# Sparse attention and a fast-multiplied MLP on one core: all steps behind batch 0 dealt in a new order

## The chip, the cores and the metric

The kernel runs on one core of one Trainium2 chip. A core has engines that run their own instruction rows side by side: TensorE (PE, with its weight loads as PEld), VectorE (DVE), ScalarE (ACT), GpSimd (POOL) and SyncE (SP). They wait for each other through semaphores, and 16 DMA engines move data for all of them. The metric is the device time of one execution in microseconds; lower is better.

## The reference

Attention with fixed sparse masks over 8 batches and 8 heads (576 tokens, 64 per head), then an MLP over all 4608 tokens. Heads 0 to 3 see the last 32 positions ("local"), heads 4 to 7 every 32nd position back from their own ("strided").

```python
B, H, S, D = 8, 8, 576, 64
scores = q @ k.T / sqrt(D)
local   = (rel >= 0) & (rel < 32)              # heads 0..3
strided = (rel >= 0) & (pos_k % 32 == pos_q % 32)  # heads 4..7
attn = softmax(where(mask, scores, -1e9))
x = (attn @ v).transpose(0, 2, 1, 3).reshape(4608, 512)
h = x @ w_in                                   # 512 -> 2048
g = h * tanh(softplus(h))                      # Mish
out = g @ w_out                                # 2048 -> 512, float32
```

## The kernel before

The tokens are cut into 9 tiles of 512 for the MLP, while attention goes by batches of 576. Stage t (there are 10) does three things at once: the first matrix product of tile t, the second product of tile t - 1, and the attention of batch t + 1. Tile 0 multiplies plainly in part; all else uses a scheme with seven products of half-size blocks instead of eight, for which DVE makes sums of blocks: `wis` and `wos` of the weights (once), `xs` of the tokens, `gs` of the activated values.

Nothing decides the order while the program runs or is built: ten strings of words (`PLANS`, from line 735) are gone through one after the other, and `do` (line 624) turns each word into instructions. An engine's row is the order in which its words stand in the strings. The order between words of different engines has no effect of its own; it decides only which instruction must wait for which. A last letter A or D names the engine, ACT or DVE; `@b` names a batch; `^` and `_` take the tile after or before the stage's own.

The words that matter here:

- `ld:..` loads k, q and v (`ks`, `kl`, `qs`, `ql`, `vs`, `vl`: s for strided, l for local heads) by DMA from POOL, `wo` and `wi` parts of the weights.
- `T:..` and `t:..`: batches 0 to 2 have q and k transposed on TensorE (T), and a copy (t) to `kTs`, `qTs`, `kTl`, `qTl`. From batch 3 on `D:..` does it by DMA transpose from SP.
- `q`, `e`, `k`, `v`, `r`: scores, exponential (ACT), mask (DVE), PV product, norm (DVE, lines 314 and 319). `sp` spreads V of the strided heads (`vs`), `sh` copies 32 rows of V of the local heads to the neighbour block (`vl`, line 182).
- `X`, `Y`, `xc`, `yc`, or by DMA transpose `y` and `V` with a copy `vc`: the attention's result transposed into `xT`.
- `x:0..3` the sums xs; `1:g` to `7:g` the seven products of column group g; `1c`, `5c` copies, `6c`, `7c` sums between them (`ee`, `hh`); `E`, `H`, `Z` the activations (lines 449, 451, 453).
- `m1` to `m7` the seven products of the second matrix, in halves; `n` and `g:1..3` the sums gs; `st` the stores from SP; `p1`, `pm`, `p2`, `oc` the plain form of tile 0.
- `hold`: a tiny copy on POOL that waits for a DMA transpose, so that the loads behind it in POOL's row don't start before.

The two lines through which every order of this change goes:

```python
        for t, plan in enumerate(PLANS):
            go(plan, t)
```

Of the kernel before, what the change touches and what calls it, by code (L numbers as in the profile page):

```python
# [45 lines left out]
def kernel(ctx, tc, q, k, v, moe_w_in, moe_w_out, out):  # L46
    nc = tc.nc
    B, H, S, D = q.shape
# [24 lines left out]
    hold = sb([1, 2], "hold")  # L73
# [9 lines left out]
    vs = sb([128, 4, CS, VD], "vs")  # L83
# [488 lines left out]
    with tc.manual_schedule():  # L572
# [158 lines left out]
        def go(plan, t=0):  # L731
            for w in plan.split():
# [26 lines left out]
            ),  # L759
            (  # L760
# [7 lines left out]
            ),  # L768
            (
# [9 lines left out]
            ),  # L779
            (  # L780
# [8 lines left out]
            ),  # L789
            (  # L790
# [8 lines left out]
            ),  # L799
            (  # L800
# [7 lines left out]
            ),  # L808
            (
# [7 lines left out]
            ),  # L817
            (
# [51 lines left out]
```

## Time and profile before

| | us |
|---|---|
| median of 3 runs | 284.81 |
| the three runs | 289.52, 284.75, 284.81 |
| the profiled execution | 284.39 |
| its span, first to last instruction | 282.6 |
| DMA queue q0 (loads from POOL) | 57808 packets, 18.30 MB |
| DMA queue q1 (transposes and stores from SP) | 40112 packets, 18.32 MB |

The profile is of one execution. "Busy" counts the time in which an engine worked on an instruction; "idle before" an instruction is the time its engine stood still ahead of it, with what ended it. Matmuls are pipelined: one that is listed with 0.27 us can follow the one ahead after 0.11. The rows themselves stand in the prediction, each where it is used.

### The profile page before, as it was taken

The numbers are of one execution on the slowest core, as the hardware profiler recorded it, in microseconds if no ns is written. First come the engines' busy times: TensorE is split into PE (matmuls) and PEld (weight loads), VectorE is DVE, ScalarE is ACT, GpSimd is POOL, SyncE is SP. The second block draws the span as 40 slices with busy tenths as digits, with TensorE's granted clock in tenths as the row PEclk, the third lists the DMA queues.
The fourth block names the chain that finished last, engine by engine and source line by source line (L and its number), as shares of the span: only waits on it lengthen the run. The fifth ranks groups of instructions, "written<-read, shape, count | busy, mean of one in ns | idle before, by whom it ended". The sixth has DMA issues, their size and how long they took to land.

```text
span 282.6 us, 7628 instructions
## 1 busy us (share of the span) xinstructions
PE 273.8 (97%) x3241; PEld 227.0 (80%) x3241; DVE 223.6 (79%) x381; ACT 189.4 (67%) x286; POOL 57.5 (20%) x78
## 2 busy tenths in 40 slices
PE   8999999999999999999999999999899999999994
PEld 3657745668989898998898889888789888888883
DVE  3679868999979886989699888886988766758761
ACT  2576884699968778788956876788376528613711
POOL 8533440250009005400720072002000000000000
PEclk9999999999999999999999999999999999999999
DMA  7999999999838978999899989999353003002104
GB/s 148 189 206 201 205 186 197 98 223 123 149 73 103 141 143 122 240 132 163 164 195 123 151 212 162 107 166 209 56 169 57 15 2 148 2 1 106 45 2 148
DMA packets 98242, 37.35 MB, mean 132 GB/s; under 512 B 79800, under 2 KB 93688, under 8 KB 98208
## 3 DMA queue, kind: packets, MB, share of 16 engines
q0 software_dynamic: 57808, 18.30, 63.9%
q1 hardware_dynamic: 40112, 18.32, 28.8%
q8 instruction: 25, 0.41, 0.6%
q10 hardware_dynamic: 288, 0.25, 0.3%
q14 instruction: 9, 0.07, 0.1%
HBM read 37.05 MB, written 9.44 MB: 164 GB/s over the span
## 4 chain that ended last, share of the span: by engine, by line
PE 84%; DVE 6%; DMA 5%; POOL 2%; issue 1%; ACT 1%; DVEq 0%; ACTq 0%; POOLq 0%
PE set L121 51%; PE ee L121 20%; PE at L121 7%; DMA w_in<-in_moe_w_in_dram 5%; PE at L302 4%; DVE xs L115 1%; DVE wis L115 1%; PE at L349 1%; DVE wos L115 1%; POOL w_in L173 0%; PE ee L349 0%; DVE qTl L112 0%; DVE ee L115 0%; DVE osb L112 0%; POOL vl L160 0%
## 5 line engine op out<-in xcount | busy, mean ns | idle before, releaser
L121 PEld LDWEIGHTS <-wis 128*128 128x128 bf16 x577 | 55.6, 98 | 10.9 <-issue 2.8
L121 PEld LDWEIGHTS <-gs 128*128 128x128 bf16 x512 | 49.2, 98 | 6.2
L121 PEld LDWEIGHTS <-gT 128*128 128x128 bf16 x448 | 42.3, 98 | 9.7 <-issue 0.3
L121 PEld LDWEIGHTS <-w_in 128*128 128x128 bf16 x436 | 41.2, 97 | 7.9 <-issue 1.0
L121 PE MATMUL set<-w_out,gT 128*128 128x256 bf16 (+1 forms) x304 | 46.3, 295 | 0.3 <-ACT gT L453 0.3
L121 PE MATMUL set<-xT,w_in 128*128 128x256 bf16 (+1 forms) x264 | 39.9, 275 | 0.6 <-DMA w_in<-in_moe_w_in_dram 0.2
L453 ACT ACTIVATE gT<-set 128x1024 bf16<-128x1024 f32 x32 | 32.8, 1024 | 11.1 <-PE set L121 10.5
L121 PE MATMUL set<-xs,wis 128*128 128x256 bf16 x256 | 37.9, 272 | 0.3 <-DVE ee L115 0.2
L449 ACT ACTIVATE gT<-ee 128x512 bf16<-128x512 f32 x35 | 20.4, 596 | 11.9 <-PE ee L121 11.1
L121 PE MATMUL set<-wos,gs 128*128 128x256 bf16 x224 | 27.6, 273 | 0.0
L115 DVE TENSOR_TENSOR ee<-set,hh 128x512 f32<-128x512 f32 x32 | 22.3, 696 | 5.8 <-PE set L121 3.4
L115 DVE TENSOR_TENSOR hh<-set,hh 128x512 f32<-128x512 f32 x32 | 21.9, 685 | 4.1 <-PE set L121 4.0
L110 ACT COPY set<-set 128x512 f32<-128x512 f32 x31 | 17.9, 579 | 9.0 <-PE set L121 8.1
L451 ACT ACTIVATE gT<-hh 128x512 bf16<-128x512 f32 x35 | 21.7, 629 | 3.2 <-DVE hh L115 3.2
L115 DVE TENSOR_TENSOR gs<-gT,gs 128x2048 bf16<-128x2048 bf16 x16 | 19.5, 1220 | 3.7 <-issue 1.7
L121 PE MATMUL ee<-xs,wis 128*128 128x256 bf16 x140 | 21.0, 272 | 0.0
L121 PE MATMUL ee<-xT,wis 128*128 128x256 bf16 x140 | 20.8, 273 | 0.0
L115 DVE TENSOR_TENSOR gs<-gT 128x2048 bf16<-128x2048 bf16 x16 | 19.4, 1214 | 1.1 <-ACT gT L451 1.1
L121 PE MATMUL set<-xs,w_in 128*128 128x256 bf16 x128 | 19.2, 272 | 0.3 <-DVE hh L115 0.3
L319 DVE TENSOR_TENSOR x_s<-at,rden 72x768 bf16<-72x768 f32 (+1 forms) x22 | 18.8, 857 | 0.8
L110 ACT COPY osb<-set 128x1024 f32<-128x1024 f32 (+1 forms) x8 | 7.7, 960 | 15.8 <-PE set L121 15.8
L110 ACT COPY hh<-ee 128x512 f32<-128x512 f32 x24 | 14.1, 588 | 5.9 <-PE ee L121 5.9
(144 smaller groups left out, 461.8 us busy)
## 6 DMA issues: line engine op xcount, KB each, us to landing
out_dram<-osb SPq DMA_DIRECT2D x17, 512.0 KB, 3.4
vl<-in_v_dram POOLq DMA_DIRECT2D x8, 288.0 KB, 12.8
w_out<-in_moe_w_out_dram POOLq DMA_DIRECT2D x4, 512.0 KB, 14.6
ks<-in_k_dram POOLq DMA_DIRECT2D x7, 288.0 KB, 12.1
qs<-in_q_dram POOLq DMA_DIRECT2D x7, 288.0 KB, 10.6
vraw<-in_v_dram POOLq DMA_DIRECT2D x7, 288.0 KB, 6.7
w_in<-in_moe_w_in_dram POOLq DMA_DIRECT2D x3, 512.0 KB, 15.4
kl<-in_k_dram POOLq DMA_DIRECT2D x10, 144.0 KB, 10.4
```

What stands on the lines that cost most here:

```text
L110: Sc.copy(out_, in_)
L115: eng.tensor_tensor(out=out_, in0=a, in1=b, op=op)
L121: PE.matmul(o, lhsT=lhsT, rhs=rhs, start=start, stop=stop, skip_group_check=True)
L302: PE.matmul(po[:, e, i, :] if kind == "l" and self.apart else po[:, (n - n0) // per, (n - n0) % per, :], lhsT=pt[0:r, c0:c0 + 128], rhs=rh ...
L319: Dv.tensor_tensor(out=xo, in0=po[0:m, :, :, 0:D], in1=rd.unsqueeze(3).to_broadcast([m, nb, per, D]), op=ALU.mult,)
L349: PE.transpose(tr[:, n * j:n * j + n], x[0:n, u:u + 2, :].rearrange("p u d -> p (u d)"), ident[0:n, 0:n],)
L449: Sc.activation(o[:, 0:2, 256:512], two(E), AF.Mish)
L451: Sc.activation(o[:, 2:4, 256:512], two(h[:, 1, :]), AF.Mish)
L453: Sc.activation(o[:, :, 0:256].rearrange("p (b u) n -> p b u n", b=2), pair[:, 0:2, :].rearrange("p b (u n) -> p b u n", u=2), AF.Mish,)
```

## The change

Strings 0 (from its middle, behind batch 0) to 9 are replaced. The same words stand in both, each as often; their order differs, and some copies and sums carry another engine letter. Counted over the program, DVE has three copies fewer and ACT three more. The rows of TensorE hold the same 3241 matmuls in another order. POOL's and SP's rows read the same before and after, word for word. In the code nothing else differs. Of the strings, a line or two is enough; this is the start of stage 6:

```diff
-                "m1:1 m1c:D m5:0 _H:3 g:1 _Z:3 ae vc:1:D@6 q:l1:F e:l1:F q:l0:A e:l0:A m5:1 m5c:A m6:0 m6:1 m6c:A g:2 "
-                "k:l0:D vc:0:D@6 x:0 q:s2:F _y:1 _y:0 _hold x:1 k:l1:D q:l2:A q:s0:A e:s0:A m3:0 e:l2:A m2:1 g:3 "
-                "e:s2:F 1:0 1c:0:A q:s1:A m7:1 x:3 m7:0 sh:D _st:1 m7c 5:0 e:s1:A v:l0:A r:l0:A am 6:0 m4:0 m4:1 "
...
+                "m5:0 m5:1 _E:3 m2:0 m2:1 _H:3 q:l1:F q:l0:A g:1 m6:0 g:2 sh:D ae e:l1:F m6:1 k:l1:D _V m5c:A m3:0 "
+                "e:l0:A q:l2:A q:s0:A q:s2:F m6c:A e:s0:A g:3 k:l0:D m7:1 e:l2:A e:s2:F q:s1:A vc:1:D@6 1:0 m7:0 "
+                "e:s1:A _y:1 _y:0 vc:0:D@6 x:0 5:0 k:l2:D 1c:0:A v:l0:A x:1 6:0 m7c m4:0 _hold m4:1 k:s0:D x:2 m3:1 "
```

DVE's row at that place, before. The two copies `xT<-ks` are vc:1 and vc:0, `gs` are the sums g, `Pl` masks, `xs` the sums x, and `vl` is sh, the copy of V rows:

```order
L115 TENSOR_TENSOR gs<-gT,gs 128x2048
L112 COPY xT<-ks 128x576
L115 TENSOR_TENSOR gs<-gT 128x2048
L280 TENSOR_TENSOR Pl_88<-Pl_88,consts_sb 128x2x480
L112 COPY xT<-ks 128x576
L115 TENSOR_TENSOR xs<-xT 128x512
L115 TENSOR_TENSOR xs<-xT,xs 128x512
L280 TENSOR_TENSOR Pl_89<-Pl_89,consts_sb 128x2x480
L115 TENSOR_TENSOR gs<-gT,gs 128x2048
L115 TENSOR_TENSOR xs<-xT,xs 128x512
L112 COPY vl_80<-vl_80 32x4x5x64
```

And now:

```order
L115 TENSOR_TENSOR gs<-gT,gs 128x2048
L115 TENSOR_TENSOR gs<-gT 128x2048
L112 COPY vl_80<-vl_80 32x4x5x64
L280 TENSOR_TENSOR Pl_89<-Pl_89,consts_sb 128x2x480
L115 TENSOR_TENSOR gs<-gT,gs 128x2048
L280 TENSOR_TENSOR Pl_88<-Pl_88,consts_sb 128x2x480
L112 COPY xT<-ks 128x576 x2
L115 TENSOR_TENSOR xs<-xT 128x512
L280 TENSOR_TENSOR Pl_90<-Pl_90,consts_sb 128x2x192
L115 TENSOR_TENSOR xs<-xT,xs 128x512
```

The copy of V rows has moved from behind both xT copies to well ahead of them, and both xT copies behind all gs sums and two masks.

ACT's row at the end of tile 0, before (`gT` rows are activations, of which the last `gT<-set_102` is Z of group 3; `set_102` is a copy 1c, `kTs` a copy t of batch 1, `Ps` an exponential):

```order
L110 COPY set_102<-set_102 128x512
L110 COPY kTs<-at 128x8x72
L451 ACTIVATE gT<-hh_68 128x2x256
L453 ACTIVATE gT<-set_103 128x4x256
L451 ACTIVATE gT<-hh_69 128x2x256
L449 ACTIVATE gT<-ee_105 128x2x256
L449 ACTIVATE gT<-ee_104 128x2x256
L451 ACTIVATE gT<-hh_68 128x2x256
L453 ACTIVATE gT<-set_102 128x4x256
L691 ACT_TABLE_LOAD
L274 ACTIVATE Ps_85<-at 72x2x144
```

And now:

```order
L110 COPY kTs<-at 128x8x72
L110 COPY set_102<-set_102 128x512
L110 COPY kTs<-at 128x8x72
L453 ACTIVATE gT<-set_103 128x4x256
L110 COPY qTs<-at 128x8x72
L451 ACTIVATE gT<-hh_69 128x2x256
L110 COPY kTl<-at 128x576
L449 ACTIVATE gT<-ee_105 128x2x256
L449 ACTIVATE gT<-ee_104 128x2x256
L451 ACTIVATE gT<-hh_68 128x2x256
L453 ACTIVATE gT<-set_102 128x4x256
L691 ACT_TABLE_LOAD
```

Three copies of transposed q and k (a second kTs, a qTs, a kTl) have come over from DVE, and one activation of `hh_68` stands earlier, ahead of this piece.

DVE's row at the start of tile 1, before (`osb` is oc, `wos` a sum of weights, `hh_68` the copy 5c:0, `vs` is sp, and `ee_104` the sum 6c:0):

```order
L112 COPY osb<-set_102 128x1024
L112 COPY qTl<-at 128x576 x2
L115 TENSOR_TENSOR wos<-w_out,wos 128x2048
L112 COPY hh_68<-ee_104 128x512
L112 COPY vs<-vraw 72x32x64
L280 TENSOR_TENSOR Ps_85<-Ps_85,consts_sb 72x2x144
L115 TENSOR_TENSOR ee_104<-set_102,hh_68 128x512
```

And now:

```order
L112 COPY osb<-set_102 128x1024
L112 COPY qTl<-at 128x576 x2
L115 TENSOR_TENSOR xs<-xT 128x512
L115 TENSOR_TENSOR wos<-w_out,wos 128x2048
L112 COPY hh_68<-ee_104 128x512
L115 TENSOR_TENSOR ee_104<-set_102,hh_68 128x512
L112 COPY vs<-vraw 72x32x64
```

The sum 6c:0 has moved ahead of the copy of V and of a mask, and an xs sum has come in before it.

More of the change, by code (lines that the diff above doesn't have):

```diff
@@ L744 @@
                 "v:l1:A@0 e:l0:C@0 r:l1:A@0 xc:1:f:A@0 v:l0:B@0 r:l0:B@0 p1:1:C:23 Y:1:f@0 p1:0:A:23 yc:1:f:A@0 "
[14 rows of a table removed]
-            ),
-            (
[7 rows of a table removed]
-            ),
-            (
[9 rows of a table removed]
-            ),
-            (
[8 rows of a table removed]
-            ),
-            (
[8 rows of a table removed]
-            ),
-            (
[7 rows of a table removed]
-            ),
-            (
[7 rows of a table removed]
-            ),
-            (
[5 rows of a table removed]
-            ),
-            (
[4 rows of a table removed]
-            ),
-            (
-                "m1:1 _H:3 m1c:0:D m5:0 _4:3 m5:1 _2:3 _Z:3 g:1 m1c:1:D m6:1 g:2 m6:0 m5c:D m3:1 m2:0 m6c:0:D m6c:1:D "
-                "g:3 m7:0 _st:0 m7:1 _st:1 m2:1 z:b:A w:b:S m7c:1 m3:0 m7c:0 m4:0 m4:1 m3c z:0:A st:1 w:0:S z:1:A "
-                "w:1:A "
[14 rows of a table added]
+            ),
+            (
[7 rows of a table added]
+            ),
+            (
[9 rows of a table added]
+            ),
+            (
[8 rows of a table added]
+            ),
+            (
[8 rows of a table added]
+            ),
+            (
[7 rows of a table added]
+            ),
+            (
[7 rows of a table added]
+            ),
+            (
[4 rows of a table added]
+            ),
+            (
[4 rows of a table added]
+            ),
+            (
+                "m1:1 m1c:1:D _3:3 _E:3 m1c:0:D m5:0 m5:1 _4:3 m5c:A _Z:3 g:1 m6:0 m6:1 m2:1 g:2 m6c:1:A m7:1 g:3 "
+                "m7c:1 m6c:0:A m2:0 _st:1 z:b:A m3:0 w:b:S m7:0 m7c:0 m3:1 m4:1 m4:0 m3c st:1 z:0:A w:0:S z:1:A w:1:A "
             ),
```

131 rows, old and new, of the table PLANS are left out of this document.

## The prediction

> **What bounds the kernel now.** I read the page's head first, then the busy time by stretch, then TensorE's waits.
>
> ```profile
> span 282.6 us, 7628 instructions
> PE 273.8 (97%) x3241; PEld 227.0 (80%) x3241; DVE 223.6 (79%) x381; ACT 189.4 (67%) x286; POOL 57.5 (20%) x78
> ...
> 80.00:108.00 28.00, 28.00 (x363) 24.36 (x361) 23.43 (x40) 22.23 (x35) 7.68 (x9) 1.00 1.11 120
> ```
>
> The columns of the last row are the stretch, its length, the busy time of PE, PEld, DVE, ACT and POOL, the granted clock, the DMA share and GB/s. TensorE (PE) is the bound: from 80 to 108 us it is busy in all 28.00 us, at a granted clock of 1.00. Its work can't be sped up by an order; only its waits can go. Their list, with total, number and longest:
>
> ```profile
> PE at L302 <- DVE vl L112: 1.2, 1, 1.2
> ...
> PE set L121 <- DVE hh L115: 0.3, 1, 0.3
> PE set L121 <- ACT gT L453: 0.3, 1, 0.3
> PE set L121 <- DVE ee L115: 0.2, 1, 0.2
> PE set L121 <- DMA w_in<-in_moe_w_in_dram: 0.2, 1, 0.2
> PE set L121 <- DVE osb L112: 0.2, 1, 0.2
> ```
>
> The three lines left out are of batch 0, which the change leaves as it was. Behind it there are these six waits, with 2.4 us of idle time (1.2 + 0.3 + 0.3 + 0.2 + 0.2 + 0.2). A wait costs more than its idle time, since the pipeline fills anew:
>
> ```profile
> 199.15 0.23 PE L302 MATMUL at<-vl,Pl 128*128 128x65 bf16 x2
> 200.61 0.46 PE L302 MATMUL at<-vl,Pl 128*128 128x65 bf16 x10 [1.24 <-DVE vl L112]
> 200.91 0.60 PE L121 MATMUL set<-xs,wis 128*128 128x256 bf16 x4
> ...
> 206.15 0.53 PE L302 MATMUL at<-vl,Pl 128*128 128x65 bf16 x12
> 206.51 0.60 PE L121 MATMUL ee<-xs,wis 128*128 128x256 bf16 x4
> ```
>
> Undisturbed, twelve matmuls of line 302 take 0.36 us from start to start (206.15 to 206.51); around the wait they took 1.76 (199.15 to 200.91). So the wait cost 1.40 for 1.24 idle, 0.16 more. All six cost 2.4 + 6 x 0.16 = 3.4 us: about what any new order can win, with some tenths more for waits too short for this list.
>
> **The change part by part.** The 3241 matmuls stay, and the rows of POOL and SP (every load, DMA transpose and store) stand in the same order before and after: no transfer passes another. What moves is the order on PE, ACT and DVE and, for some copies, which of ACT and DVE makes them. The sum is made against the profiled execution, 284.39 us (span 282.6 and 1.8 around it), 0.42 under the median of 284.81.
>
> Stage 6 (about 190 to 203 us). The PV products of batch 7 (`v:l0`) waited for a copy of V rows (`sh`, vl) that stood late in DVE's row:
>
> ```profile
> 190.49 1.22 DVE L115 TENSOR_TENSOR gs<-gT,gs 128x2048 bf16<-128x2048 bf16 x1
> 194.04 0.72 DVE L112 COPY xT<-ks 128x576 bf16<-128x576 bf16 x1 [2.33 <-DMA ks<-x_s]
> 194.68 1.22 DVE L115 TENSOR_TENSOR gs<-gT 128x2048 bf16<-128x2048 bf16 x1
> 195.81 0.65 DVE L280 TENSOR_TENSOR Pl<-Pl,consts_sb 128x960 bf16<-128x960 bf16 x1
> 196.38 0.71 DVE L112 COPY xT<-ks 128x576 bf16<-128x576 bf16 x1
> 197.12 0.42 DVE L115 TENSOR_TENSOR xs<-xT 128x512 bf16<-128x512 bf16 x1
> ...
> 200.07 0.48 DVE L112 COPY vl<-vl 32x1280 bf16<-32x1280 bf16 x1
> ...
> L332 SPq DMA_TRANSPOSE ks<-x_s x2: 1348/1628/1909, 188.3 to 216.6; - x2
> DMA to landing us min/median/max: 3.7/4.6/5.6
> ...
> q8 instruction: 25, 0.41, 0.6%
> ```
>
> DVE stood 2.33 us before the first xT copy (`vc:1`), until the DMA transpose of x_s issued at 188.3 landed, and ten instructions later came the vl copy. That transpose took 5.6 us, its twin at 216.6 took 3.7; during the first one an instruction fetch (one packet of queue q8) ran, during the second none. In the new row sh stands ahead of both xT copies, right behind the sums g:1 and g:2. To see whether that suffices I laid TensorE's steps end to end in the new order, each with its length of before and without waits. On that scale 4:3 ends at 187.2, ACT's last activations of the tile (1.03, then two of about 0.64) end near 189.8, so g:1 starts there and sh ends near 192.7, five us ahead of v:l0 (197.6): the wait on vl is gone, -1.40. Late next is `5:0`, which needs vc:1, vc:0 and x:0 in a row: g:1 (1.22), g:2 (1.22), sh (0.48), a mask (0.65), g:3 (1.22), a mask (0.65), two xT copies (0.71 each), x:0 (0.42) make 7.3 us from 189.8, to 197.1, and 5:0 stands at 197.1 on the same scale. That just meets, so I put 0.2 against it: -1.2. The transpose itself now waits for a norm (`r:s2`) that DVE reaches behind a gs sum, about 1.2 us later than before; even with 5.6 us to landing it is there about 1.7 us before vc:1. If that cover fails, 5:0 waits.
>
> The Trainium skill, page "Runtime: NRT & Kernel Launch", section "Instruction fetch mechanics", says that an engine's instructions are fetched in blocks of 16 KiB (256 instructions) over a queue of its own, and that crossing a block is mostly hidden. For the engine the trace agrees: q8's 25 packets with 0.41 MB are 16 KB each, and none of TensorE's waits above is laid to them. For the transposes it does not: 5.6 against 3.7 us. Were fetches hidden from them too, the lateness would be chance, and the sum would be that of rival D below; I go by the row.
>
> Tile 0 (21 to 40 us). Rows at the two waits that can go, and the end of the stretch:
>
> ```profile
> 30.02 0.60 PE L121 MATMUL set<-xs,w_in 128*128 128x256 bf16 x4 [0.30 <-DVE hh L115]
> 35.56 1.02 PE L121 MATMUL set<-w_out,gT 128*128 128x512 bf16 x4 [0.28 <-ACT gT L453]
> 40.05 0.39 PE L121 MATMUL at<-qTl,kTl 64*128 64x96 bf16 x10
> ...
> 30.93 1.03 ACT L453 ACTIVATE gT<-set 128x1024 bf16<-128x1024 f32 x1
> 31.83 0.64 ACT L451 ACTIVATE gT<-hh 128x512 bf16<-128x512 f32 x1
> 34.48 1.02 ACT L453 ACTIVATE gT<-set 128x1024 bf16<-128x1024 f32 x1 [0.39 <-PE set L121]
> ...
> 28.92 0.46 DVE L112 COPY kTs<-at 128x576 bf16<-128x576 bf16 x1 [0.38 <-PE set L121]
> 29.29 0.68 DVE L115 TENSOR_TENSOR hh<-set,hh 128x512 f32<-128x512 f32 x1
> ```
>
> The weights w_in land at 21.0 as before. Followed from there with the durations of these rows and their neighbours (an instruction of ACT or DVE follows its forerunner about 0.1 us before that one's end, 30.93 + 0.90 = 31.83): the kTs copy leaves DVE, so the hh sum (`7c:2`) starts at 28.8 instead of 29.29 and `4:2`, which waited at 30.02, at 29.5; the last product of the tile ends at 33.7 instead of 34.2. ACT takes over three copies (kTs, qTs, kTl), and its last activation (L453) ends at 35.7 instead of 35.5, but a step on the other bank now stands before its reader, so the 0.28 wait goes. A wait of 0.4 comes in: `q:s0` behind the second kTl copy on DVE, until 35.0. The score step of 40.05 comes out at 39.45: -0.6. Bounds: -1.2 if q:s0 need not wait and ACT keeps up, +0.6 if ACT and DVE do not overlap their neighbours by that 0.1.
>
> Tile 1's start:
>
> ```profile
> 59.81 1.14 DVE L112 COPY vs<-vraw 72x2048 bf16<-72x2048 bf16 x1
> 61.08 0.68 DVE L115 TENSOR_TENSOR ee<-set,hh 128x512 f32<-128x512 f32 x1
> ```
>
> The vs copy (`sp`, 1.14) and a mask stood before the ee sum (`6c:0`) for which TensorE idled 0.2 us. Now the sum is ahead of them, with one 0.42 xs sum added before it; TensorE has one step (0.4) less in between. 1.14 is more than 0.42 + 0.4 + 0.2, so the wait goes with its refill: -0.4. The osb wait stays: the steps about it stand as before.
>
> New waits elsewhere. The trace of before can't show them. Several sums have less room in the new order; the tightest, `6:g` to `7:g`, has two to three steps of about 0.4 us between, 0.9 to 1.3 us, and needs 0.16 + 0.70. Bounds: 0, and 1.4 (the largest wait there was). Nearer 0, since the chain fits where DVE is free: +0.3. The last stage keeps its tail: last matmul, two osb copies, two stores.
>
> Sum: -1.2 - 0.6 - 0.4 + 0.3 = -1.9, so 282.5 against the profiled execution; with half of the 0.42 to the median, 282.7 us.
>
> **The rivals.** A: waits move instead of going. V's transpose, issued later, meets a fetch and lands behind vc:1's turn: about 1.0 of the 1.4 comes back before 5:0; tile 0 gives nothing, since ACT now has three more copies before its last activation; new waits are 0.7. -1.4 + 1.0 - 0.4 + 0.7 = -0.1: 284.3 to 284.7. For it speaks DVE's row in stage 6, which only just meets; against it the 1.7 us of cover.
>
> B: slower, by the DMA loop. On POOL a hold waits for a batch's last transpose, then the next batch's loads go out, then its four transposes:
>
> ```profile
> POOL hold L689 <- DMA qTs<-qs: 57.0, 3, 20.6
> ...
> 135.74 0.18 POOL L689 COPY hold<-qTs 1x2 bf16<-1x2 bf16 x1 [19.37 <-DMA qTs<-qs]
> 163.79 0.18 POOL L689 COPY hold<-qTs 1x2 bf16<-1x2 bf16 x1 [20.61 <-DMA qTs<-qs]
> ...
> 129.35 2.00 SPq L189 DMA_TRANSPOSE kTl<-kl  x1
> ...
> kTl<-kl SPq DMA_TRANSPOSE x1, 4.4
> ...
> 134.93 0.39 PE L121 MATMUL at<-qTl,kTl 64*128 64x96 bf16 x10
> ```
>
> The loop turns in 163.79 - 135.74 = 28.05 us, as long as a stage of TensorE. kTl landed at 129.35 + 4.4 = 133.8, 1.1 us before its reader. If TensorE runs ahead while the loop doesn't, and each of three turns meets one more fetch (5.6 - 3.7 = 1.9), readers wait 3 x 1.9 - 1.1 = 4.6: 287.3. It decides once transposes are over 1.1 us later against TensorE than now. Against it: the rows of SP and POOL are unmoved, batch 2's results are ready earlier, so the loop starts earlier too, and in stages 4 to 6 the score steps stand further back in TensorE's row.
>
> C: all six waits go and none comes: 284.4 - 3.4 = 281.0, or some tenths less.
>
> D: the lateness of the x_s transpose was chance. Then the runs outside the profile mostly lack the 1.40 wait, there is nothing to win in stage 6, and the sum is -0.6 - 0.4 + 0.3 = -0.7: 283.7. For it speaks that there is one such pair to compare; against it the fetch that lies inside the late one.
>
> **How the numbers follow.** My forecast (281.3 to 283.4) has 0.50, A 0.20, D 0.13, B 0.10, C and better 0.07. 280.9 to 285.6 leaves out most of B and a little of C, under 0.2. A measurement of this kernel can tell about 2% from no change. 2% faster is under 279.1, 5.3 us, more than all waits cost (3.4 and some tenths): 0.01. 2% slower is over 290.5, beyond B's price: 0.03.
>
> **What would show it.** In the new profile: no wait of TensorE on vl, and vc:1 on DVE without its 2.33 us; the score step of 40.05 near 39.5; no ee wait near 60. I am wrong if TensorE waits on xs or ee before 5:0 in stage 6, on the kTl copy for more than 0.5 us near 35, or on kTl, qTl, kTs or qTs from stage 3 on.

## The result, and the profile after

| | before | changed |
|---|---|---|
| median of 6 runs, us | 285.71 | 283.51 |
| ratio, 95% interval | | 0.9935 (0.991 to 0.996) |
| profiled execution, us | 284.39 | 283.36 |
| its span, us | 282.6 | 281.6 |

The changed kernel is 0.65% faster: within 2%, as forecast, and 0.1 points short of the forecast's own ratio (282.7 / 284.81 = 0.9926). A second measurement (experiment 5) gave 0.9928 (0.9895 to 0.9962). Yet the two profiled executions are only 1.03 us apart, not 1.9. Both facts have to be explained. Ratios, means and spreads in this document leave out runs more than 1.5% above the fastest of their kernel, most of which show a lower granted clock, and of the profiles of experiments 5 and 10, which are of such runs, only the list of waits is read.

The list of TensorE's waits in the changed kernel, with total, number and longest:

```profile
PE at L121 <- DVE wis L577: 1.2, 1, 1.2
PE ee L202 <- DMA qs<-in_q_dram: 0.7, 1, 0.7
PE at L121 <- DVE kTl L112: 0.3, 1, 0.3
PE ee L202 <- DMA ks<-in_k_dram: 0.3, 1, 0.3
PE set L121 <- DVE osb L115: 0.3, 1, 0.3
PE set L302 <- ACT Pl L274: 0.3, 1, 0.3
PE set L121 <- DVE osb L112: 0.2, 1, 0.2
```

The 1.2 us on vl is gone, and so are the waits on gT, hh, ee and w_in. Behind batch 0 two are new: kTl (tile 0, forecast) and osb of line 115 (stage 4, not forecast). By stretch, TensorE's idle time is the second column (length) less the third (busy). Before:

```profile
18.00:41.00 23.00, 22.00 (x263) 14.91 (x262) 19.29 (x41) 17.40 (x25) 8.96 (x12) 1.00 1.34 201
41.00:72.00 31.00, 30.37 (x417) 21.58 (x416) 28.21 (x46) 23.47 (x40) 7.31 (x8) 1.00 1.28 157
72.00:191.00 119.00, 119.00 (x1476) 104.60 (x1474) 101.05 (x167) 93.71 (x139) 28.83 (x37) 1.00 1.25 151
191.00:203.00 12.00, 10.76 (x142) 9.15 (x135) 9.51 (x16) 7.70 (x13) 1.46 (x2) 1.00 0.76 153
```

And in the changed kernel:

```profile
18.00:41.00 23.00, 22.40 (x277) 15.45 (x276) 18.42 (x40) 20.08 (x30) 7.84 (x11) 1.00 1.35 201
41.00:72.00 31.00, 30.47 (x412) 21.91 (x411) 28.37 (x48) 23.09 (x39) 7.27 (x8) 1.00 1.31 167
72.00:191.00 119.00, 118.53 (x1450) 103.61 (x1449) 101.92 (x167) 88.20 (x132) 28.86 (x37) 1.00 1.21 147
191.00:203.00 12.00, 12.00 (x162) 10.22 (x160) 10.61 (x18) 10.31 (x18) 1.45 (x2) 1.00 0.85 167
```

Idle time fell from 1.00 to 0.60 in tile 0 and from 1.24 to 0 in stage 6, and rose from 0 to 0.47 in the long middle. Idle time leaves out refills and waits that the pipeline half covers, so I also added up, over all matmuls, what the start-to-start time exceeds the median for the same pair of shapes in both traces. This lost time is, before and after: up to 17.5 us, where both kernels do the same, 4.7 and 4.3; 17.5 to 41 us 3.2 and 2.2, of which 0.35 before is a late landing of w_in; 41 to 57 us 1.3 and 1.6; 57 to 72 us 1.6 and 1.3; 72 to 191 us 4.3 and 5.2; 191 to 203 us 1.8 and 0.7; behind it 0.3 and 0.5. The sums differ by 1.4 us and the spans by 1.0; the measure doesn't see what a pair of shapes costs that only one order has. The 0.3 of batch 0 and the 0.35 of w_in lie in steps that the change didn't move, so that part of the gap between the profiles isn't the order's. Stage 6 of the changed kernel on DVE, with x:0 and TensorE's `5:0` behind the two xT copies:

```profile
192.11 1.22 DVE L115 TENSOR_TENSOR gs<-gT,gs 128x2048 bf16<-128x2048 bf16 x1 [1.84 <-ACT gT L451]
193.26 1.22 DVE L115 TENSOR_TENSOR gs<-gT 128x2048 bf16<-128x2048 bf16 x1
194.51 0.48 DVE L112 COPY vl<-vl 32x1280 bf16<-32x1280 bf16 x1
195.00 0.66 DVE L280 TENSOR_TENSOR Pl<-Pl,consts_sb 128x960 bf16<-128x960 bf16 x1
195.83 1.23 DVE L115 TENSOR_TENSOR gs<-gT,gs 128x2048 bf16<-128x2048 bf16 x1 [0.17 <-PE set L121]
196.97 0.65 DVE L280 TENSOR_TENSOR Pl<-Pl,consts_sb 128x960 bf16<-128x960 bf16 x1
197.54 1.34 DVE L112 COPY xT<-ks 128x576 bf16<-128x576 bf16 x2
198.91 0.42 DVE L115 TENSOR_TENSOR xs<-xT 128x512 bf16<-128x512 bf16 x1
...
199.72 0.60 PE L121 MATMUL ee<-xs,wis 128*128 128x256 bf16 x4
...
L332 SPq DMA_TRANSPOSE ks<-x_s x2: 1340/1344/1349, 190.3 to 215.5; - x2
DMA to landing us min/median/max: 3.7/4.4/5.1
```

The transpose of x_s still takes 5.1 us instead of 3.7. But it lands at 190.3 + 5.1 = 195.4, and its reader vc:1 has its turn at 197.54: 2.1 us of room, where vc:1 had stood waiting before.

### The profile page after: what moved, and what is told of

Read it like the earlier page. It is cut to its first block, busy times and chain, and to the rows that moved or that the text cites. A ratio compares the mean times of both kernels' runs of the same rounds, so it can differ in the third digit from the quotient of the medians.

```text
span 281.6 us, 7619 instructions
## 1 busy us (share of the span) xinstructions
PE 273.3 (97%) x3241; PEld 226.6 (80%) x3241; DVE 221.8 (79%) x378; ACT 190.3 (68%) x289; POOL 58.0 (21%) x78
## 4 chain that ended last, share of the span: by engine, by line
PE 83%; DMA 8%; DVE 4%; ACT 2%; issue 1%; POOL 0%; DVEq 0%; ACTq 0%; POOLq 0%
PE set L121 50%; PE ee L121 20%; PE at L121 7%; DMA ks<-in_k_dram 6%; PE at L302 4%; DMA qs<-in_q_dram 2%; DVE ee L115 1%; PE ee L202 1%; DVE gs L115 1%; DVE x_s L319 1%; PE at L349 1%; ACT set L110 1%; DVE Ps L280 0%; PE ee L349 0%; PE at L202 0%
## 5 line engine op out<-in xcount | busy, mean ns | idle before, releaser
L121 PE MATMUL set<-w_out,gT 128*128 128x256 bf16 (+1 forms) x304 | 45.6, 295 | 0.0
L110 ACT COPY set<-set 128x512 f32<-128x512 f32 x34 | 19.6, 577 | 14.2 <-PE set L121 13.1
L121 PE MATMUL ee<-wos,gT 128*128 128x256 bf16 x128 | 16.3, 273 | 0.0
L274 ACT ACTIVATE Ps<-at 72x1008 bf16<-72x1008 f32 (+1 forms) x15 | 11.6, 770 | 6.8 <-PE at L121 6.8
```

Of the source, the lines that this page charges most:

```text
L110: Sc.copy(out_, in_)
L121: PE.matmul(o, lhsT=lhsT, rhs=rhs, start=start, stop=stop, skip_group_check=True)
L274: Sc.activation(pt[0:n, :, 0:c], ps[0:n, :, o:o + c], AF.Exp, scale=scale)
```

## The experiments

Ratios are to the kernel before, measured on the same chip in the same call, with 95% intervals.

### Where the gain lies (experiments 1, 2, 3 and 6)

The strings of both kernels can be joined at a stage's edge: one kernel's words up to there, then the other's words that are still to do, in their order.

```diff
 e1_head_new:       stages 0 and 1 changed
-                   stages 2 to 9 changed
+                   stages 2 to 9 as before
 e2_tail_new:       stages 6 to 9 changed
-                   stages 0 to 5 changed
+                   stages 0 to 5 as before
 e3_head_and_tail:  stages 0, 1, 6 to 9 changed
-                   stages 2 to 5 changed
+                   stages 2 to 5 as before
 e6_only_middle:    stages 2 to 5 changed
-                   stages 0, 1, 6 to 9 changed
+                   stages 0, 1, 6 to 9 as before
```

> The new order up to the end of stage 1, the old one from stage 2 on. By the comparison of the two profiles the new order gains 1.0 us between 17.5 and 41 us and about 0.1 net from there to 72. If that is the order's own doing: 0.9 to 1.3 us less than the kernel before (ratio 0.995 to 0.997), the 0.28 and 0.30 waits of tile 0 gone, a wait on the kTl copy of about 0.3 near 34.5, and the vl wait of 1.2 still there in stage 6. If the gain of tile 0 was one execution's chance (its DMA landings): 0 to 0.3 us less.

> The old order up to the end of stage 5, the new one from stage 6 on. If the wait of the PV products on the vl copy (1.40 us with its refill) is in every execution of the kernel before: 0.9 to 1.4 us less (ratio 0.995 to 0.997), no wait on vl, none before 5:0 over 0.2. If the late transpose of x_s was one execution's chance: 0 to 0.3 us less. If the new stage 6 needs its own stages before it (sums ready earlier), a new wait of 0.3 or more before 5:0 and a gain of at most 0.7.

> New order in stages 0 and 1 and from 6 on, the old one in stages 2 to 5. By the profiles the new order of 72 to 191 us adds 0.9 us in many small waits (5.2 against 4.3 lost beyond the undisturbed pace). If these are the order's own: 2.0 to 2.6 us less than the kernel before (ratio 0.991 to 0.993), that is 0.5 to 0.9 less than the changed kernel, and the sum of the two kernels with only the head and only the tail. If they are chance, or if the gains do not add: the time of the changed kernel (1.85 less, ratio 0.9935) or above.

> Old order in stages 0 and 1 and from 6 on, the new one in stages 2 to 5. If the new middle gives the transposes room: slack of 2.4 us or more at batch 5 and 4 us or more at batch 6 (the kernel before: 1.1 and 1.8), no wait on kTl, scatter of undisturbed times under 1.5 us where the kernel before has 3.4, so that the mean of the undisturbed times falls by 0.3 to 0.8 us although the fastest runs are 0 to 0.7 slower. If the middle is only worse by its small waits: ratio 1.001 to 1.003, scatter as before. The vl wait of stage 6 stays in both cases.

| | ratio | fastest and mean run, us | spread (standard deviation) |
|---|---|---|---|
| before (first call) | | 284.08, 285.49 | 0.99 |
| head only | 0.9985 (0.9948 to 1.0021) | 283.10, 285.01 | 1.21 |
| tail only | 0.9915 (0.9878 to 0.9951) | 282.77, 283.25 | 0.67 |
| head and tail | 0.9915 (0.9886 to 0.9944) | 282.16, 283.09 | 0.54 |
| middle only | 1.006 (1.0024 to 1.0096) | 286.36, 287.13 | 0.71 |

The tail alone brings more (0.85%) than the 0.4 to 0.5% that its one wait is worth, and in the mean it is as fast as the changed kernel (283.41 in the second measurement). So the gain that the mean runs can tell lies in stages 6 to 9. The head's gain is there in the fastest runs (1.0 us) but not certain in the mean; its profile has the expected waits (hh and gT gone, 0.3 on the kTl copy, 1.4 on vl). Head and tail without the new middle fit the 0.991 to 0.993 that was expected of them, but the interval also holds the changed kernel's 0.9935, so the middle's harm is not proved by this. The middle alone missed both forecasts of time by far, though no wait on a transpose of k or q stands in its profile, as expected. That profile has waits of 0.35, 0.29 and 0.22 where the new stage 5 meets the old stage 6, and there the largest wait on vl so far:

```profile
203.43 0.46 PE L302 MATMUL at<-vl,Pl 128*128 128x65 bf16 x10 [1.56 <-DVE vl L112]
```

Its sums come out later than the old stage 6 expects. A stage's order has no price of its own; it depends on what stands behind it.

### One word moved, and one moved back (experiments 4 and 8)

```diff
 e4_only_sh_moved: before, stage 6
-... g:1 _Z:3 ae vc:1:D@6 ... m7:0 sh:D _st:1 m7c ...
+... g:1 _Z:3 ae sh:D vc:1:D@6 ... m7:0 _st:1 m7c ...
 e8_vc_at_its_old_place: changed kernel, stage 6
-... g:1 m6:0 g:2 sh:D ... k:l1:D _V m5c:A ... q:s1:A vc:1:D@6 1:0 ...
+... g:1 _V vc:1:D@6 m6:0 g:2 sh:D ... k:l1:D m5c:A ... q:s1:A 1:0 ...
```

> The kernel before with one word moved: sh, the copy of V rows, now stands ahead of the xT copy vc:1 in DVE's row, in the time DVE stood still. If DVE's standstill for the transpose and sh behind it are the whole cause: TensorE's wait on vl goes and nothing follows, 1.2 to 1.4 us less (ratio 0.995 to 0.996), with vc:1's own wait of about 1.9 us on DVE still there. If the whole of stage 6 had to be dealt anew: at most 0.5 us less, with a new wait right behind (before 5:0 or on m7c). If the late transpose was one execution's chance: 0 to 0.2 less.

> The changed kernel with the transpose of x_s and its copy vc:1 put back to right behind g:1, ahead of g:2 and sh in DVE's row. If DVE's standstill behind vc:1 is the cause of the old wait, and the room for it the gain of stage 6: DVE stands 2 to 4 us at vc:1, sh, the masks and g:3 come later by as much, TensorE waits 1.2 to 2.5 us in stage 6 (on gs, vl or m7c), ratio to the kernel before 0.996 to 1.002, that is 1 to 2 us above the changed kernel. If other moves of the new stage 6 bring the gain: within 0.4 us of the changed kernel.

Moving sh alone gave 0.9976 (0.994 to 1.0012). The profiled run was the slowest of the ten that count, with two waits on kTl ahead of stage 6, shown further below. TensorE no longer waits on vl, but in the profile of e4 DVE stands 2.84 us, and everything behind vc:1 is late, down to the sum m7c (osb):

```profile
193.68 0.48 DVE L112 COPY vl<-vl 32x1280 bf16<-32x1280 bf16 x1
197.00 0.72 DVE L112 COPY xT<-ks 128x576 bf16<-128x576 bf16 x1 [2.84 <-DMA ks<-x_s]
...
202.94 0.68 DVE L115 TENSOR_TENSOR osb<-set,o 128x512 f32<-128x512 f32 x1
...
203.67 1.03 PE L121 MATMUL set<-w_out,gs 128*128 128x256 bf16 x8 [1.40 <-DVE osb L115]
```

The wait went from the first reader behind the standstill to a later one. Putting vc:1 back early in the changed kernel, with the transpose that it reads (`_V`), gave 1.001 (0.9968 to 1.0052), against 0.9928 for the changed kernel in the same call; the mean runs are 2.2 us apart (285.57 and 283.41). In the profile of e8 DVE stands 2.32 us again, and TensorE waits for g:2 and for x:0:

```profile
195.24 0.72 DVE L112 COPY xT<-ks 128x576 bf16<-128x576 bf16 x1 [2.32 <-DMA ks<-x_s]
...
197.15 1.05 PE L121 MATMUL set<-wos,gs 128*128 128x256 bf16 x8 [0.42 <-DVE gs L115]
...
201.12 0.61 PE L121 MATMUL ee<-xs,wis 128*128 128x256 bf16 x4 [1.18 <-DVE xs L115]
```

So what counts in stage 6 is that vc:1 stands behind work that can go on while the transpose flies; the place of sh is the smaller part.

### The changed kernel again, and the transpose made later (experiments 5, 9 and 10)

```diff
 e9_before_transpose_later, e10_after_transpose_later:
+    lag = sb([128, 4, D], "lag")
...
             elif f == "V":
+                if b == 6:
+                    for i in range(4):
+                        nc.sync.dma_start(lag[0:SU, i], x_s[0:SU, i])
                 at[b].xs_dma()
```

> The changed kernel once more, for a second profile of it and its scatter beside the others'. If its order leaves the DMA transposes 2.4 to 5.6 us before their readers in every execution: no wait of TensorE on kTl, qTl, kTs or qTs, undisturbed times within 1 us of each other, ratio 0.990 to 0.995. If the slack of its profile was chance: a wait on kTl of about 1 us in stages 4 or 5 here too, and a scatter of 2 to 3 us as the kernel before has. Its small waits (m4:0 on osb near 143, 0.49; the 0.28 near 127.7) come again at the same places if they are the order's own, elsewhere if chance.

> The kernel before, with four small DMA copies of rows of x_s into a tile that nobody reads, issued from SP ahead of the first transpose of x_s: about 0.5 us each, so this transpose and what follows it on SP start about 2 us later. In the old row vc:1 has no room (it starts when the transpose lands), so each microsecond goes through: DVE stands 3.5 to 4.8 us instead of 2.33, TensorE waits 2.5 to 3.5 us on vl instead of 1.24, and the time is 1.2 to 2.3 us above the kernel before (ratio 1.004 to 1.008). If DVE's standstill is not what the time hangs on: within 0.4 us of it.

> The changed kernel with the same four copies ahead of the same transpose. In the new row the transpose lands 2.2 us before vc:1's turn (195.37 against 197.54), so about 2 us are swallowed: no wait of TensorE before 5:0 above 0.5 us, and 0 to 0.6 us above the changed kernel (ratio to the kernel before 0.992 to 0.996). If the new order has no such room, or its gain is another: 1.2 to 2.3 us above the changed kernel, as for the old order.

The changed kernel's second measurement gave 0.9928, with ten of its eleven runs between 282.90 and 283.78 us and one at 284.89. In its profile the same small waits stand (kTl 0.3, osb 0.2), and none on a transpose of k or q.

The four copies took SP 3.06 us, more than the 2 I had put. The kernel before went to 1.010 (1.0062 to 1.0138), mean run 288.03 against 285.40: 2.6 us slower, more than the 1.2 to 2.3 that were expected. The changed kernel with the same copies measured 0.9937 (0.9905 to 0.9969), mean 283.09, not to be told from the changed kernel (283.41). The old row passes lateness through, the new one swallows it. The profile of e9, DVE's row and TensorE's, and then the stretches behind (length, busy times, and PEclk third from the end):

```profile
196.76 0.72 DVE L113 COPY xT<-ks 128x576 bf16<-128x576 bf16 x1 [3.58 <-DMA ks<-x_s]
...
203.34 0.71 PE L303 MATMUL at<-vl,Pl 128*128 128x65 bf16 x10 [2.25 <-DVE vl L113]
...
203.00:204.00 1.00, 0.66 (x11) 0.65 (x11) 0.97 (x2) 0.00 (x0) 0.00 (x0) 0.66 0.81 134
204.00:207.00 3.00, 3.00 (x17) 2.16 (x15) 2.72 (x7) 0.00 (x0) 0.00 (x0) 0.54 0.03 6
207.00:212.00 5.00, 5.00 (x57) 4.53 (x55) 3.72 (x8) 2.60 (x5) 0.00 (x0) 1.00 0.28 107
```

After the 2.25 us wait the granted clock is 0.54 for three microseconds, which costs another 3.00 x 0.46 = 1.4 us. The expectation did not have this.

This can explain the gap between profile and runs. Kernels in which vc:1 has room (tail only, head and tail, the changed kernel twice, and experiments 10, 11 and 12) have runs with a spread of 0.2 to 0.7 us. Those in which it starts when the transpose lands (before, and experiments 1, 4, 7, 8 and 9) spread by 1.0 to 1.6; the middle-only kernel, at 0.7, is the exception. Between the fastest runs of one call the changed kernel gains 0.93 us (283.83 to 282.90), like the two profiles; between the means 2.06 (285.47 to 283.41). I put the other 1.1 us down to runs in which the transposes came later than in the profile. Those runs have no trace, so this step is argued from the spread and from experiments 9 and 10. A mean granted clock near 0.99, the mark of such a long wait in e9's profile (0.991), was seen in 14 of 104 runs of the kernel before and in none of 19 of the changed kernel; of the twelve runs of experiment 11, whose vc:1 has room, one shows it too.

The traces show a second place without room. With the old stages 2 to 5, TensorE waited on the DMA transpose `kTl` of batch 5 or 6 in five profiles of seven. The lines are of experiments 1, 2, 4 (two waits), 7 and 9:

```profile
PE set L121 <- DMA kTl<-kl: 1.0, 1, 1.0
...
PE set L121 <- DMA kTl<-kl: 0.6, 1, 0.6
...
PE at L121 <- DMA kTl<-kl: 1.1, 1, 1.1
PE set L121 <- DMA kTl<-kl: 1.0, 1, 1.0
...
PE at L121 <- DMA kTl<-kl: 1.2, 1, 1.2
...
PE set L122 <- DMA kTl<-kl: 0.5, 1, 0.5
```

The profile of the kernel before and that of experiment 3 have no such wait, and neither has any of the seven profiles with the new stages 2 to 5. So the one profile of before was a lucky one there. Its lost time of 4.3 us between 72 and 191 us is the lowest of the seven with the old stages (4.3 to 6.2, mean 5.2); five profiles with the new stages have 4.9 to 5.9, mean 5.2. What the new middle loses in small waits it seems to win back on kTl. This doesn't explain the tail's gain, since the tail-only kernel kept the old stages 2 to 5 and such a wait of 0.6 us.

### The fetches moved (experiment 7)

```diff
         def unread(n, to):
+            if to is BANK["a"]:
+                for i in range(8):
+                    mm(to[:, 64 * i:64 * i + 64], wis[:, 0, 0, 0, 0:128], wis[:, 0, 0, 0, 0:64], True)
+                return
             for _ in range(n):
                 mm(to, wis[:, 0, 0, 0, 0:128], wis[:, 0:2, 0, 0, :], True)
```

> The kernel before, with the ten 512-column fillers on bank a at the start and one more cut into eight of 64 columns each: 84 matmuls (168 instructions of TensorE) more, no time of their own. Every later instruction fetch of TensorE comes 168 instructions earlier, about 8 us in stage 6 (192.1 to about 184). If the fetch is what holds the transpose of x_s: it lands in 3.6 to 4.6 us instead of 5.6, DVE's standstill before vc:1 is under 1.3 instead of 2.33, TensorE's wait on vl is gone or under 0.4, and kTl or qTl of batch 7, which the fetch now meets, take 0.7 to 2 us longer; the transpose qTl at 127 (5.5, fetch at 130.4) comes down to about 4. If the lateness belongs to the place in the queue: the transpose of x_s takes 5.4 to 6.3 again, with no fetch in it, and the vl wait stays at 1.0 to 1.5.

Eleven of the twelve fillers stand at the start; the twelfth, in stage 7, also readies bank a for a product that is added to it, and cut in pieces it no longer does, so, read from the code, one column group of tile 7 comes out otherwise. (The Trainium skill, page "PSUM — Partial Sum Buffer", section "The four PSUM rules", says that a product's first matmul clears the write marks of the whole bank; that fits, but no run here tested it.) Ahead of that nothing but the fillers is touched. The fetch of 192.1 now comes at 187.6, 2.3 us ahead of the transpose of x_s. Its line and TensorE's wait in the profile of e7:

```profile
L332 SPq DMA_TRANSPOSE ks<-x_s x2: 1349/1706/2062, 189.9 to 217.2; - x2
...
  DVE xT L112: 1.4, 1
...
DMA to landing us min/median/max: 3.7/4.2/4.6
...
201.18 0.46 PE L302 MATMUL at<-vl,Pl 128*128 128x65 bf16 x10 [0.34 <-DVE vl L112]
```

4.6 us instead of 5.6, the standstill 1.4 instead of 2.33 (under 1.3 was expected), the wait 0.34 instead of 1.24. The fetch that moved to 187.6 fell into kTl of batch 7, which took 5.4 instead of 3.9. One part missed: qTl near 129 was not freed (6.2 us), since another fetch came into it at 132.8. With its fetches elsewhere the kernel measured 1.0051 (1.0006 to 1.0096), slower by 1.6 us in the mean.

All profiles together agree. Of the 264 DMA transposes of k, q and x_s in 12 profiles (those but experiments 5 and 10), 149 had no fetch from half a microsecond ahead of the issue to the landing: 3.5 to 4.7 us, median 3.9. 51 had one that began 2 us or more after the issue: median 5.4, up to 6.5. Where every fetch began within the first microsecond, the median was 3.8 (25 transposes). Why a fetch makes a transpose late, no run shows.

### The copies back on DVE (experiment 11)

```diff
-t:ks0:A:A@1 ... t:qs0:A:A@1 ... t:kl1:A:A@1
+t:ks0:A:D@1 ... t:qs0:A:D@1 ... t:kl1:A:D@1
```

> The changed kernel with the three copies of tile 0 that went to ACT (kTs, qTs, kTl of batch 1) made by DVE again, at the same places. If moving them is what gains in tile 0: a wait of TensorE of 0.3 us or more on hh or kTl between 27 and 36 comes back, the score step of batch 1 (39.4 with the copies on ACT) starts 0.4 to 1.0 us later, and the time is 0.3 to 0.8 us above the changed kernel. If only the order of the steps matters there: within 0.2 us of the changed kernel.

Ratio 1.0005 (0.9968 to 1.0043): mean run 285.69, 2.3 us above the changed kernel's 283.41, three times what was expected. In the profile of e11 DVE stands still for the transposes of qs, which are TensorE's own, and the sum 6c:3 behind that copy is late:

```profile
30.97 0.46 DVE L112 COPY qTs<-at 128x576 bf16<-128x576 bf16 x1 [1.18 <-PE at L202]
31.34 0.68 DVE L112 COPY hh<-ee 128x512 f32<-128x512 f32 x1
32.06 0.70 DVE L115 TENSOR_TENSOR ee<-set,hh 128x512 f32<-128x512 f32 x1
...
32.81 0.60 PE L121 MATMUL set<-xs,wis 128*128 128x256 bf16 x4 [1.51 <-DVE ee L115]
```

So in tile 0 the new order loses without the new engine letters; the letters without the order were not tried.

### Two small waits mended (experiment 12)

```diff
 changed kernel, stage 0 and stage 4
-... sw:2:2:3:D 1:1 ... 1:2 x:2 5c:1:A 6c:1 ...
+... x:2 sw:2:2:3:D 1:1 ... 1:2 5c:1:A 6c:1 ...
-... v:l0:A r:l0:A m4:0 m4:1 6:0 m3:1 ...
+... v:l0:A r:l0:A m3:1 m4:0 m4:1 6:0 ...
```

> The changed kernel with two words moved: in stage 4 the half product m3:1 goes ahead of m4:0 (which waited 0.49 us with its refill for m7c on DVE near 143), and in tile 0 the sum x:2 goes ahead of a weight sum (7:1 waited 0.28 near 24.6 for 6c:1 behind it on DVE). If these small waits are the order's own: both gone, nothing new in their place, 0.5 to 0.8 us below the changed kernel (ratio to the kernel before 0.989 to 0.991). If each wait only moves to the next step, or if they were one execution's chance: within 0.2 us of the changed kernel.

The changed kernel's row (first) and this one's at stage 4:

```profile
142.99 1.91 PE L121 MATMUL set<-w_out,gs 128*128 128x256 bf16 x16 [0.33 <-DVE osb L115]
```

```profile
142.27 1.04 PE L121 MATMUL ee<-wos,gT 128*128 128x256 bf16 x8
143.15 1.91 PE L121 MATMUL set<-w_out,gs 128*128 128x256 bf16 x16
```

Both waits are gone; the profiled execution took 282.81 against 283.36. The ratio, 0.9936 (0.9909 to 0.9963), can't tell it from the changed kernel; the 0.989 to 0.991 that were expected did not come. Its profiled execution is the shortest of all, but only its lead over the kernel before is certain.

## Why the prediction came out right

**The bound and the ceiling** stood: TensorE is busy 97% of the span before and after, and only waits changed. The largest gain of a mean run, 2.4 us (head and tail), stays under the 3.4.

**Stage 6**, forecast -1.2: the lost time fell by 1.1, with vc:1 no longer waiting. Late next was to be `5:0`, just met; x:0 ended 0.4 us ahead of it (199.33 and 199.72, both over 2 us later than on the forecast's scale). The cover of the transpose, forecast as 1.7 us, was 2.1. The cause held too: with no fetch inside, the same transpose took 4.6 us. On the Trainium skill's rule (page "Runtime: NRT & Kernel Launch", section "Instruction fetch mechanics", that crossing a block of instructions is mostly hidden) the runs agree for TensorE and disagree for transposes in flight, by the 5.4 against 3.9 us above. Rival D, that the lateness was chance, falls with that, and with the waits on vl in all three profiles that have the old stage 6 unaltered (1.24, 1.4 and 1.56). A small misreading in the forecast has no effect: the vl copy stood nine instructions behind vc:1, not ten.

**Tile 0**, forecast -0.6: about -0.65 by the lost time, once the 0.35 of a late w_in is taken off. The forecast wait on the kTl copy came, with 0.3 us. The score step of 40.05 came at 38.96 instead of the forecast's 39.45:

```profile
34.56 0.24 PE L121 MATMUL at<-qTs,kTs 64*128 64x72 bf16 x4 [0.34 <-DVE kTl L112]
...
38.96 0.39 PE L121 MATMUL at<-qTl,kTl 64*128 64x96 bf16 x10
```

Of these 1.09 us, 0.33 and 0.35 are batch 0's and w_in's, so 0.4 is left for the order. One pair of profiles is a weak measure here: the lost time of 17.5 to 41 us is 2.2 to 3.2 in four profiles with the new head unaltered and 3.2 to 3.7 in six with the old one. Their means, 2.8 and 3.5, bear the term out; the mean runs don't show it with certainty (experiment 1). The term's weakest assumption, that ACT has time for three more copies, was right, and more hung on it than I had seen (experiment 11).

**Tile 1's start**, forecast -0.4: -0.3, the wait on ee gone.

**New waits elsewhere**, forecast +0.3: about +1.3 against the one profile of before (0.2, 0.9 and 0.2 in the three stretches). By that measure the term was mis-sized. I looked for the tightest chain of sums and took it for the measure; what came was a queue on DVE (m7c behind g:3 and a mask, 0.49 with its refill) and several waits of 0.15 to 0.3 us behind ACT and DVE that the list of waits doesn't show. The bound of 1.4 held them. Against all profiles of the old middle the 0.9 is made up for by the waits on kTl, which the sum, read from a profile without them, could not have.

**What was left out** is room, the time from a transfer's landing to its reader's turn. Rival B's mechanism, transposes that come late, was priced only as a danger to the changed kernel. It is a cost of the kernel before: experiment 9 shows it passing lateness on, experiment 10 the new order swallowing it, and the waits on kTl show it in the traces. Without a gain of about 1.1 us in the mean run that the sum doesn't have, the extra waits would have left a saving near 1.0. That the forecast's -2.1 came out as -2.1 is therefore in part luck: new waits put too low against the profile, and room that was left out, of opposite sign. How the 1.1 us divide between vc:1 and kTl stays open. For k and q the room is seen in the traces: the first score step on kl of batch 5 and of batch 6 starts 2.4 and 4.8 us after its operands have landed, against 1.1 and 1.8 before.

Rival A (waits move) fell with the absent wait before 5:0, though experiment 4 shows it to be what happens when sh alone moves. Rival C (all waits go and none comes) fell with the new waits on the kTl copy and on osb.

## What to carry to other kernels

A reader that stands in its engine's row right where its transfer lands has no room, and each later landing reaches the bound engine; put work that is ready between the two, and price that room from several executions, not from one. When a wait is removed by moving its victim, look at what stands next behind the same standstill. A new order can earn small waits of its own (0.9 us over the long middle here), so give them a term, and size it by the queues on the helper engines and not by the tightest chain alone.

## What the runs showed of the hardware

A DMA transpose into which an instruction fetch falls 2 us or more after its issue lands about 1.5 us later (median 5.4 against 3.9), and where the fetches fall depends on the number of TensorE's instructions ahead: 77 tiny matmuls more at the start changed which transposes came late 180 us further on (experiment 7).

A wait of TensorE of 2.25 us was followed by a granted clock of 0.54 for 3 us; after waits of 1.24 to 1.56 us none was seen. The Trainium skill, page "TensorE: Matmul & The Clock Gate", section "What's actually happening", says that the clock falls to half after an idle window of about 3.4 us. The half agrees; here, in one profile, a shorter wait was enough.
